# Turning the normalised rows of blocks 1 to 3: TensorE transposes, or a way over memory and 32x32 turns on VectorE

## The chip, the core and the metric

The kernel runs on one core of a Trainium2 chip. The metric is device time in microseconds (us), from runs without a profiler; the profile comes from one separate profiled execution. The engines are PE (TensorE: matmuls and transposes; PEld is its weight load, which overlaps), DVE (VectorE), ACT (ScalarE), POOL (GpSimd) and SP (SyncE, which here only issues DMAs). Each engine works through its own instructions in order; they wait for one another on semaphores.

## What is computed

One block of a transformer on 2048 tokens (S) with 512 features (D), all in float32:

```python
xn = _layernorm(x, axis=-1)
s = _A_ref(xn, A_wqkv, A_wo)
g = _silu(_B_ref(xn, B_w_gate, B_w_up, B_w_down))
return x + s * g
```

`_A_ref` is attention with 32 heads of 16 features and no mask; `_B_ref` is `(silu(x @ w_gate) * (x @ w_up)) @ w_down` with 1792 hidden features. Both take the same normalised rows `xn`. The matrix products contract over the features, and TensorE contracts over the partitions (the 128 rows of on-chip memory), so `xn` is needed with its features on the partitions: it has to be turned.

## The kernel before

**Two phases.** A prologue (lines 446 to 797, about the first 160 us) normalises x, turns it and makes queries, keys and values. Then comes a long loop over attention units (from line 821), into which the feed-forward products and the output projection are dealt as filling work. The change lies in the prologue.

**Blocks, tiles and slots.** The 2048 tokens are 4 blocks (`NB`) of 512 (`TB`); a block has 4 tiles (`NT`) of 128 tokens. For each block b the loop at lines 685 to 762 runs through 12 slots (`n`): 8 of `feature_tile` (line 632), which make 128 rows of queries or keys for all 512 tokens, and 4 of `value_tile` (line 644), which make the values of 128 tokens. Block 0 has the values first (slots 0 to 3), blocks 1 to 3 have them last (slots 8 to 11). Each slot is 12 matmuls, because every operand is split into a high and a low fp32r part and three of the four products are kept (`project`, line 577). The result lies in one of four PSUM buffers `ps`.

**What a feature slot issues.** ACT squares and copies `ps` (lines 637 and 638), DVE takes the difference (line 639), and SP stores both halves, 512 KB, to `q_d` or `k_d` (line 641). `parts` has four buffers. A value slot has one ACT copy into `vt` (line 659).

**The turn of the next block.** While block b is worked on, block b+1 is prepared. `load_x` (line 464) has SP load four tiles of x into `xin`; `stats(t)` (line 530) and `rates` (line 540) make mean and scale on DVE, with one square root on ACT; `norm(t)` (line 551) writes the normalised tile `xn`, 128 tokens by 512 features, into a buffer of tag `ga`, which has two. `turn` (line 558) then issues four TensorE transposes of 128x128 into a PSUM bank, and `split_x` (line 563) has ACT cast the result to the high part (line 565) and DVE take the difference (line 568). They land in `xt[b % 2]`, which the matmuls of the next block read: a feature slot reads all four tiles. After tile 3 POOL stores `xt` to `xt_d` (line 574) for the feed-forward phase. Which slot does what stands in lines 728 to 737: in blocks 1 and 2, x is loaded in slot 1, stats in slots 2 to 5, rates in slot 5, norms in slots 6 to 9, turns in slots 7 to 10. In block 0 the x tiles are loaded in slot 2, stats are made in slots 2 and 3, and rates in slot 4.

**What sets the order.** The order within each engine is the order of the program text (`manual_schedule`, line 53). The Tile layer adds the semaphore waits: a reader waits for its writer, also through DRAM, and a new tile in a buffer waits until all uses of the old one are done. A DMA's waits stand on the engine that issues it, so everything behind it on that engine waits too.

**Other users of what the change touches.** `th` and `wdr` are tags with one buffer of 128x512 floats each (pool `one`). In the prologue `wdr` receives the first rows of the down weights (`load_wd(0)`, line 701, read after the prologue), and `th` serves tile 0 of block 0 (`xf`, line 604) and later the feed-forward products. `load_gu` (line 123) loads gate and up weights, two DMAs of 256 KB, in slots 6 and 7 of block 2. In block 0, `load_w`, `high_w` and `low_w` (lines 690 to 695) still load and split weights, and `copy_fx` (line 667) has ACT copy the turned block 0 into `fx`. `flush` (line 680) reduces the squares; it stands in slot 8 of blocks 1 to 3 and in slot 0 of block 1.

Of the kernel before, what the change touches and what calls it, by code (L numbers as in the profile page):

```python
# [9 lines left out]
F32 = mybir.dt.float32  # L10
# [9 lines left out]
P = 128  # L20
S = 2048
D = 512
# [4 lines left out]
TB = S // NB  # L27
NT = TB // P
# [22 lines left out]
def tile_block(ctx: ExitStack, tc: tile.TileContext, x, wqkv, wo, w_gate, w_up, w_down, out):  # L51
# [3 lines left out]
    mm, act, dve, sp, pool = nc.tensor.matmul, nc.scalar.activation, nc.vector, nc.sync, nc.gpsimd  # L55

    dram = ctx.enter_context(tc.tile_pool(name="dram", bufs=1, space=DRAM))
# [4 lines left out]
    xt_d = dram.tile([NB, 2, P, DT, TB], F32, name="xt_d")  # L62
    g_d = dram.tile([S, D], F32, name="g_d")
    o_d = dram.tile([DT, NB, P, TB], F32, name="o_d")

    const = ctx.enter_context(tc.tile_pool(name="const", bufs=1))
    one = ctx.enter_context(tc.tile_pool(name="one", bufs=1))
    two = ctx.enter_context(tc.tile_pool(name="two", bufs=2))
# [51 lines left out]
    gu, wdr = {}, {}  # L120


    def load_gu(i):
        f = i % NF
        raw = two.tile([P, DC, P], F32, tag="gur", name="gur")
        for j, w in enumerate((w_gate, w_up)):
            sp.dma_start(raw[j * HALF:(j + 1) * HALF], w[:, f * P:(f + 1) * P].rearrange("(c p) f -> p c f", p=HALF))
        gu[i] = [raw]
# [9 lines left out]
    def load_wd(i):  # L138
        raw = one.tile([P, D], F32, tag="wdr", name="wdr")
        sp.dma_start(raw, w_down[(i % NF) * P:(i % NF + 1) * P])  # L140
        wdr[i] = raw
# [304 lines left out]
    with ExitStack() as pro:  # L446
# [10 lines left out]
        def load_tile(t):  # L457
            if t:
                sp.dma_start(xin[:, t % NT], x[t * P:(t + 1) * P])
            else:  # L460
                for engine, w in zip((nc.scalar, sp), wide):
                    engine.dma_start(xin[:, t, w], x[t * P:(t + 1) * P, w])

        def load_x(b):
            for t in range(NT):
                load_tile(b * NT + t)
# [11 lines left out]
        def load_w(m):  # L478
            wraw[m] = two.tile([P, DT, P], F32, tag=("gur", "guh", "gul")[len(wraw) % 3], name="wraw")
            if m < 8:  # L480
                src = wqkv[:, m * P:(m + 1) * P].rearrange("(c p) f -> p c f", p=P)
            else:
                c = m - 8
                src = wqkv[c * P:(c + 1) * P, 2 * D:3 * D].rearrange("p (c f) -> p c f", f=P)
            sp.dma_start(wraw[m], src)
# [6 lines left out]
        def high_w(m):  # L492
            nc.scalar.copy(parts_w(m)[0], wraw[m])

        def low_w(m):
            hi, lo = parts_w(m)
            return pool.tensor_sub(lo, wraw[m], hi.bitcast(F32))
# [30 lines left out]
        xn = {}  # L528
# [22 lines left out]
        def norm(t):  # L551
            xn[t] = two.tile([P, D], F32, tag="ga", name="xn")
            return dve.tensor_scalar(xn[t], xin[:, t], mv[:, t, 0:1], rs[:, t:t + 1], op0=ALU.subtract, op1=ALU.mult)
# [4 lines left out]
        def turn(t):  # L558
            for c in range(DT):
                turn_one(acc[t % 2], t, c)  # L560
            return acc[t % 2].rearrange("p (c f) -> p c f", f=P)

        def split_x(b, t, av, between=None):
            hi, lo = (xt[b % 2][j][:, :, t * P:(t + 1) * P] for j in range(2))
            nc.scalar.copy(hi, av)
            if between:
                between()
            dve.tensor_sub(lo, av, hi.bitcast(F32))  # L568

        def turn_x(b, t, between=None):  # L570
            split_x(b, t, turn(t), between)
            if t == NT - 1 and b:
                for j in range(2):
                    pool.dma_start(xt_d[b, j], xt[b % 2][j].bitcast(F32))

# [109 lines left out]
        for b in range(NB):  # L685
            more = b + 1 < NB
            slots = [(feature_tile, m) for m in range(8)]
            slots = [(value_tile, t) for t in range(NT)] + slots if b == 0 else slots + [(value_tile, t) for t in range(NT)]
            for n, (make, i) in enumerate(slots):
                if b == 0:  # L690
                    if n + 5 < 12:
                        load_w(worder[n + 5])
                    if n >= 2 and n + 2 < 12:
                        high_w(worder[n + 2])
                        low_w(worder[n + 2])
                if n == (1 if b else 2) and more:
                    load_x(b + 1)
                if b == 2 and n in (6, 7):
                    load_gu(n - 6)
                if b == 2 and n == 8:  # L700
                    load_wd(0)
                if not more and n == 2:
                    split_gu(0)
                    for bank in acc:
                        dve.memset(bank, 0.0)
                if not more and n in (1, 3):
                    load_k(0, n // 2)
                if not more and n == 5:
                    load_q(0)
                if not more and n == 6:  # L710
                    for c in range(2):
                        load_v(0, c)
                if b == 0 and n == 1:
                    norm(2)
                    norm(3)
                made = make(b, i)
                if b == 0 and n == 2:
                    split_x(0, 0, xf)
                if b < 2 and 0 <= 12 * b + n - 3 < 16:
                    copy_fx(12 * b + n - 3)  # L720
                if n == 0 and b == 1:
                    flush(0)
                if make is feature_tile:
                    pend.append(made)
                if b == 0 and n == 11:
                    ring(0, 2, one)
                    queries(0, one)
                if more:
                    for t in range(NT):
                        if n == 2 + (t if b else t // 2):  # L730
                            stats(t)
                    if n == (5 if b else 4):
                        rates(0, NT)
                    if 6 <= n < 10:
                        norm(n - 6)
                    if 7 <= n < 11:
                        turn_x(b + 1, n - 7)
                if n == 8 and b:
                    flush(b)
                if not more and n == 8:  # L740
                    dve.reduce_max(pk, peak, axis=AX.X)
                    dve.tensor_add(sm, pk[:, 0:1], pk[:, 1:2])
                if not more and n == 9:
                    tops = pps.tile([P, 512], F32, tag="ps", name="tops")
                    nc.tensor.transpose(tops[0:1, :P], sm, ident)
                    dve.reduce_max(s4, tops[0:1, :P], axis=AX.X)
                    dve.tensor_scalar(s4, s4, 0.51, None, op0=ALU.mult)
                    dve.tensor_scalar(flag, s4, LIMIT, None, op0=ALU.is_le)
                    dve.tensor_scalar(sel[:, :NG * NB], row[:, :NG * NB], s4, None, op0=ALU.mult)
                    for h in range(2):  # L750
                        dve.tensor_copy(selq[:, h * HALF:h * HALF + 1], s4)
                    fill(3 * DC)
                    low, high = [pps.tile([P, 512], F32, tag="ps", name="low") for _ in range(2)]
                    mm(high[:2 * NG * NB, :8], sel, row[:, :8], start=True, stop=True, skip_group_check=True)
                    mm(low[:HALF + 2, :8], selq, row[:, :8], start=True, stop=True, skip_group_check=True)
                    act(shift, high[:2 * NG * NB, 0:1].to_broadcast([2 * NG * NB, 512]), AF.Copy, scale=-1.0)
                    for h in range(2):
                        two_rows = slice(h * HALF, h * HALF + 2)
                        act(qst[0][two_rows], low[two_rows, None, 0:1].to_broadcast([2, 2, 512]), AF.Copy, scale=-1.0)
                    for j in range(4):  # L760
                        pool.dma_start(sh_d[:, j * 512:(j + 1) * 512], shift.bitcast(F32))
                    fast = nc.values_load(flag, min_val=0, max_val=1)


        with tc.If(fast < 1):
            with tc.tile_pool(name="gen", bufs=1) as gen:
                for h in range(2):
                    pool.memset(qst[0][h * HALF:h * HALF + 2].bitcast(F32), 0.0)
                for g in range(NG):
                    for b in range(NB):  # L770
# [3 lines left out]
                        for j in range(NB):  # L774
                            load_k(g, j, j % 2)
                            for i in range(4 * NT):
                                h, t = divmod(i, NT)
                                ps = pps.tile([P, 512], F32, tag="ps", name="ps")
                                r = slice(h % 2 * HALF, h % 2 * HALF + NROW)
# [41 lines left out]
    for u in range(units):  # L821
        g, b = divmod(u, NB)
        q = qst[u % 2]
        for kp in range(steps):
            now = u * steps + kp
            probs = []
            for i in range(2):
# [4 lines left out]
                for j in range(2):  # L832
                    for h in range(2):
                        r = slice(h * HALF, h * HALF + NROW)
# [41 lines left out]
    turned = []  # L876
# [65 lines left out]
```

## Time and profile before

| What | Value |
|---|---|
| median of 3 runs | 1436.54 us (1436.37 to 1437.82) |
| the profiled execution, whole time | 1437.19 us |
| its span, first to last instruction | 1435.4 us |
| granted TensorE clock, mean | 0.999 |
| instructions | 26786 |
| DMA over the span | 149.15 MB, mean 104 GB/s |
| DMA, 0 to 170 us | 39.13 MB, mean 230 GB/s |

How to read the rows that follow. In a timeline a row has the start in us from the span's start, the duration, the engine, the line of the kernel, the operation, output<-inputs, shapes and the number of merged instructions; in brackets the idle time before it and what ended it. SPq is SP issuing: the duration is that of the issue, not of the transfer. Where several are merged, the duration runs from the first one's start to the last one's end. In the rows by group the fields are count | busy us, mean ns of one | idle us before, and what ended it. Rows that begin with A:B are stretches: the width, the granted clock, the share of time in which the 16 DMA engines were busy, and GB/s; where the PE is shown, its busy time and count stand ahead of the clock. "DMA packets" and "q1" tell the packets of a stretch, their MB and the time they took as a share of 16 engines. DMA issues are given with KB each and the median time from issue to landing.

### The profile page before, as it was taken

Reading aid. Unit: us, or ns where it says so; the run is one execution under the profiler, and the core shown is the slowest. Engines: PE = TensorE matmul, PEld = TensorE weight load, DVE = VectorE, ACT = ScalarE, POOL = GpSimd, SP = SyncE. Lnnn points to the kernel's source line nnn. Section 1 sums busy time; section 2 is a strip of 40 time slices with the busy share of each in tenths; the row PEclk is TensorE's granted clock in tenths of the full one; section 3 lists DMA queues with packets and bytes.
Section 4 is the critical chain, followed back from the end, with each engine's and each line's share of the span. In section 5 each row is a group of like instructions: output and inputs, shape, how many; then the busy total and the mean of one; then the engine's idle time right before and its main releaser. Section 6 shows DMA issues by size and latency. Waiting matters only on the chain.

```text
span 1435.4 us, 26786 instructions
## 1 busy us (share of the span) xinstructions
PE 1428.2 (99%) x11221; PEld 803.6 (56%) x11221; DVE 535.0 (37%) x886; ACT 1112.2 (77%) x1236; POOL 89.6 (6%) x103
## 2 busy tenths in 40 slices
PE   9999999999999999999999999999999999999998
PEld 7778655555555555555555555555555555555555
DVE  5543344112523342134323431243344422243665
ACT  6733688888888888788888888888888887888764
POOL 4200200000000000000000000000000000000154
PEclk9999999999999999999999999999999999999999
DMA  7778652032274321142553320342824210412552
GB/s 222 264 242 253 157 119 64 17 96 60 64 153 119 97 65 34 38 105 71 111 134 90 94 49 12 79 104 58 177 79 121 65 42 12 101 30 78 196 183 104
DMA packets 127668, 149.15 MB, mean 104 GB/s; under 512 B 12604, under 2 KB 79676, under 8 KB 126772
## 3 DMA queue, kind: packets, MB, share of 16 engines
q1 hardware_dynamic: 122196, 126.71, 34.5%
q0 software_dynamic: 4912, 20.12, 3.8%
q8 instruction: 91, 1.49, 0.5%
q10 hardware_dynamic: 432, 0.52, 0.1%
q14 instruction: 37, 0.30, 0.1%
HBM read 107.20 MB, written 40.11 MB: 103 GB/s over the span
## 4 chain that ended last, share of the span: by engine, by line
PE 88%; DVE 0%; issue 0%; DVEq 0%
PE acc L356 33%; PE bankx L174 32%; PE score L835 20%; PE banky L174 3%; DVE y L889 0%; PE acc L882 0%; DVE y L895 0%; PE score L882 0%; PE banky L882 0%; DVEq L938 0%; DVE rl L886 0%; DVEq L895 0%
## 5 line engine op out<-in xcount | busy, mean ns | idle before, releaser
L837 ACT ACTIVATE pr<-score 128x1024 f32<-128x1024 f32 x1024 | 993.2, 1023 | 223.0 <-PE score L835 222.4
L356 PE MATMUL acc<-pr,vst 128*17 128x512 f32 x4096 | 489.2, 595 | 0.0
L835 PE MATMUL score<-qst,kst 50*128 50x512 f32 x2048 | 352.1, 421 | 0.0
L835 PEld LDWEIGHTS score<-qst,kst 50*128 50x128 f32 x2048 | 177.1, 184 | 263.7 <-ACT pr L837 225.7
L174 PE MATMUL bankx<-fx,guh 64*128 64x512 f32 x896 | 288.8, 392 | 0.1
L174 PE MATMUL banky<-fx,guh 64*128 64x512 f32 x896 | 288.8, 392 | 0.0
L356 PEld LDWEIGHTS acc<-pr,vst 128*17 128x17 f32 x4096 | 94.0, 96 | 234.6 <-issue 233.8
L204 DVE SCALAR_TENSOR_TENSOR ga<-th,bankx 128x512 f32<-128x512 f32 x56 | 38.5, 688 | 445.3 <-ACT th L203 445.3
L174 PEld LDWEIGHTS bankx<-fx,guh 64*128 64x128 f32 x896 | 165.7, 185 | 34.5 <-issue 0.9
L174 PE MATMUL banky<-fx,gul 64*128 64x512 f32 x448 | 175.3, 391 | 0.0
L174 PE MATMUL bankx<-fx,gul 64*128 64x512 f32 x448 | 175.3, 391 | 0.0
L174 PEld LDWEIGHTS banky<-fx,guh 64*128 64x128 f32 x896 | 165.7, 185 | 2.8
L174 PE MATMUL banky<-wd,hh 64*128 64x512 f32 x672 | 166.7, 389 | 0.0
L174 PE MATMUL bankx<-wd,hh 64*128 64x512 f32 x672 | 166.6, 389 | 0.0
L174 PEld LDWEIGHTS bankx<-wd,hh 64*128 64x128 f32 x672 | 124.0, 185 | 26.1
L174 PEld LDWEIGHTS banky<-wd,hh 64*128 64x128 f32 x672 | 124.0, 185 | 1.4
L174 PEld LDWEIGHTS bankx<-fx,gul 64*128 64x128 f32 x448 | 82.9, 185 | 17.8
L174 PEld LDWEIGHTS banky<-fx,gul 64*128 64x128 f32 x448 | 82.8, 185 | 1.4
L588 PE MATMUL ps<-xt,wh 128*128 128x512 f32 x256 | 80.9, 397 | 0.1
L222 DVE COPY facc<-bankx 128x512 f32<-128x512 f32 x16 | 11.1, 692 | 171.1 <-PE banky L174 150.3
L135 DVE TENSOR_TENSOR gul<-gur,guh 128x1024 fp32r<-128x1024 f32 x56 | 68.6, 1225 | 2.1
L588 PEld LDWEIGHTS ps<-xt,wh 128*128 128x128 f32 x256 | 47.8, 188 | 11.8 <-DVE xt L568 0.5
(161 smaller groups left out, 1019.1 us busy)
## 6 DMA issues: line engine op xcount, KB each, us to landing
gur<-in_B_w_gate_dram SPq DMA_DIRECT2D x56, 256.0 KB
gur<-in_B_w_up_dram SPq DMA_DIRECT2D x56, 256.0 KB
wdr<-in_B_w_down_dram SPq DMA_DIRECT2D x56, 256.0 KB
kst<-k_d SPq DMA_DIRECT2D x192, 64.0 KB
qst<-q_d SPq DMA_DIRECT2D x192, 64.0 KB
fx<-xt_d SPq DMA_DIRECT2D x24, 512.0 KB
q_d<-parts SPq DMA_DIRECT2D x16, 512.0 KB
k_d<-parts SPq DMA_DIRECT2D x16, 512.0 KB
```

The costliest lines, as they stand in the source:

```text
L135: dve.tensor_sub(lo, raw, hi.bitcast(F32))
L174: mm(bank, lhs[h], rhs[h], start=start, stop=stop)
L204: dve.scalar_tensor_tensor(ga, th, 1.0, bankx, op0=ALU.add, op1=ALU.mult)
L222: dve.tensor_copy(facc[:, t], bankx)
L356: mm(a[h * 32:h * 32 + DH + 1], v[:, kt % CT, h * (DH + 1):(h + 1) * (DH + 1)], probs[2 * i + h // 2][:, h % 2], start=kt == 0, stop=kt == ...
L588: mm(ps, w, a[:, c], start=n == 0, stop=n == 3 * DT - 1)
L835: mm(score[j][:, h], k[r, j, kc * P:(kc + 1) * P], q[r, j], start=True, stop=True)
L837: exps.append(act(pr, score[j], AF.Exp, scale=0.25))
```

## The change

The transposes of blocks 1 to 3 are taken from TensorE. Each normalised tile is stored to a new DRAM tensor `xn_d`, in the slot of its `norm`. One slot later four loads (`spread`), 32 partitions each, bring it back with its 32x32 squares already in their turned places: 128 bytes (32 floats) are contiguous in a run, 512 runs to a load. Then DVE turns every 32x32 square where it stands (`turn_over`), and `split_x` works from on-chip memory instead of PSUM. The buffers are `th` and `wdr` in turn for the loaded tile and `ga` for the turned one. The four tiles of block 0 keep the TensorE path.

The slots move: in blocks 1 and 2, x is loaded in slot 0, stats are in slots 1 to 3, rates in slot 3, norms and stores in slots 4 to 7, loads of the squares at the head of slots 5 to 8, turns at the end of slots 7 to 10 as before. In block 0, norms move from slots 6 to 9 to slots 4 to 7. `load_wd(0)` moves to slot 0 of block 3.

```diff
+    xn_d = dram.tile([S, D], F32, name="xn_d")
...
         def turn_x(b, t, between=None):
             split_x(b, t, turn(t), between)
-            if t == NT - 1 and b:
+        xb = {}
+
+        def spread(b, t):
+            xb[t] = one.tile([P, D], F32, tag=("th", "wdr")[t % 2], name="xb")
+            src = xn_d[b * TB + t * P:b * TB + (t + 1) * P].rearrange("(a j) (c g i) -> g j c a i", j=32, g=4, i=32)
+            for g in range(4):
+                dst = xb[t][g * 32:(g + 1) * 32].rearrange("j (c a i) -> j c a i", a=4, i=32)
+                sp.dma_start(dst, src[g])
+
+        def turn_over(b, t):
+            turned = two.tile([P, D], F32, tag="ga", name="turned")
+            dve.transpose(turned, xb.pop(t))
+            split_x(b, t, turned.rearrange("p (c f) -> p c f", f=P))
+            if t == NT - 1:
                 for j in range(2):
                     pool.dma_start(xt_d[b, j], xt[b % 2][j].bitcast(F32))
...
-                if n == (1 if b else 2) and more:
+                if n == (0 if b else 2) and more:
                     load_x(b + 1)
+                if 5 <= n < 9 and more:
+                    spread(b + 1, n - 5)
                 if b == 2 and n in (6, 7):
                     load_gu(n - 6)
-                if b == 2 and n == 8:
+                if b == 3 and n == 0:
                     load_wd(0)
...
                     for t in range(NT):
-                        if n == 2 + (t if b else t // 2):
+                        if n == (1 + (t + 1) // 2 if b else 2 + t // 2):
                             stats(t)
-                    if n == (5 if b else 4):
+                    if n == (3 if b else 4):
                         rates(0, NT)
-                    if 6 <= n < 10:
-                        norm(n - 6)
+                    if 4 <= n < 8:
+                        norm(n - 4)
+                        r = (b + 1) * TB + (n - 4) * P
+                        sp.dma_start(xn_d[r:r + P], xn[n - 4])
                     if 7 <= n < 11:
-                        turn_x(b + 1, n - 7)
+                        turn_over(b + 1, n - 7)
```

## The prediction, made before the changed kernel was run

> **What bounds the kernel now.** I read first the busy times, then the stretch that the change touches (the prologue, 0 to about 160 us) on TensorE's timeline.
>
> ```profile
> PE 1428.2 (99%) x11221; PEld 803.6 (56%) x11221; DVE 535.0 (37%) x886; ACT 1112.2 (77%) x1236; POOL 89.6 (6%) x103
> 22.10 0.62 PE L588 MATMUL ps<-xt,wh 128*128 128x512 f32 x2
> 24.88 0.64 PE L588 MATMUL ps<-xt,wh 128*128 128x512 f32 x2
> 33.25 0.60 PE L556 MATMUL acc<-ident,xn 128*128 128x128 f32 x4
> 36.48 0.60 PE L556 MATMUL acc<-ident,xn 128*128 128x128 f32 x4
> 46.16 1.01 PE L588 MATMUL ps<-xt,wh 128*128 128x512 f32 x2
> 83.25 0.62 PE L588 MATMUL ps<-xt,wh 128*128 128x512 f32 x2
> 119.20 0.62 PE L588 MATMUL ps<-xt,wh 128*128 128x512 f32 x2
> ```
>
> TensorE is busy throughout, so time taken from it is gained and any wait put on it is lost. A slot (one `make`) takes 24.88 - 22.10 = 2.78 us; one with a turn of four transposes takes 36.48 - 33.25 = 3.23. A turn costs 0.45. Blocks 1, 2 and 3 begin at 46.16, 83.25 and 119.20. **Removed:** 12 turns, 12 x 0.45 = 5.4 us. This is all that the change can gain.
>
> **The new path.** A block has 12 slots, 12 x 2.78 = 33.4 us without turns, and the next block's first slot needs all four tiles turned. Each tile now goes: norm on DVE, store of `xn` on SP, four gathers on SP which read what that store wrote, a 32x32 turn on DVE, cast on ACT, difference on DVE. SP issues in program order. It stands still before tile t's gathers until tile t's store has landed; the stores of `parts` and the next tile's `xn` store queue behind. So the tiles follow one another round a loop on SP, and I cost that loop. These are SP's issue times:
>
> ```profile
> 2.64 0.43 SPq L459 DMA_DIRECT2D facc<-in_A_x_dram  x1
> 3.11 0.43 SPq L485 DMA_DIRECT2D wraw<-in_A_wqkv_dram  x1
> 63.25 8.73 SPq L641 DMA_DIRECT2D k_d<-parts  x4
> 88.47 4.43 SPq L459 DMA_DIRECT2D facc<-in_A_x_dram  x4
> 102.45 0.72 SPq L127 DMA_DIRECT2D gur<-in_B_w_gate_dram  x1
> 103.22 0.66 SPq L127 DMA_DIRECT2D gur<-in_B_w_up_dram  x1
> ```
>
> One issue occupies SP 0.47 us (3.11 - 2.64), for a weight tile in 512 runs as for an x tile in 128 rows; a gather has 32 x 16 = 512 runs. Four: 1.9 us. Behind a full queue one takes 4.43 / 4 = 1.1, four 4.4; that is the upper bound.
>
> Packets, in a stretch with 512-byte ones (18 to 22 us) and one with 2 KB ones (65 to 81 us):
>
> ```profile
> DMA packets 925, 0.46 MB, mean 114 GB/s; under 512 B 32, under 2 KB 925, under 8 KB 925
> q1 hardware_dynamic: 925, 0.46, 39.9%
> DMA packets 934, 1.80 MB, mean 112 GB/s; under 512 B 64, under 2 KB 64, under 8 KB 933
> q1 hardware_dynamic: 933, 1.78, 29.4%
> ```
>
> 0.399 x 4 us x 16 / (925 - 32) = 28.6 ns for 512 bytes, and 0.294 x 16 x 16 / (933 - 64) = 87 ns for 2 KB. The line through them gives 14 ns at 128 bytes; a run that costs as much as a 512-byte one gives 28.6. A tile has 2048 runs, 128 for each of 16 engines: 1.8 to 3.7 us. I take 2.6, between them, so that the queue lags the issue (1.9) by 0.7. The Trainium skill (DMA: Bandwidth & Descriptors, Specifications) puts line rate at 512 bytes and up and says that shorter transfers are read, modified and written; no 128-byte run is in this trace, and by the rule a tile would take at least the 3.7, the whole 12 x 1.1 = 13 us more.
>
> Landing of a store that SP waits for:
>
> ```profile
> 0.76 0.39 SPq L462 DMA_DIRECT2D facc<-in_A_x_dram  x1
> 3.54 0.75 DVE L537 BATCH_NORM_STATS2 st<-facc 128x6 f32<-128x256 f32 x2 [0.79 <-DMA facc<-in_A_x_dram]
> 73.50:74.00 0.50, 1.00 0.79 287
> 74.00:74.50 0.50, 1.00 0.00 0
> xt_d<-xt POOLq DMA_DIRECT2D x6, 1024.0 KB, 5.3
> ```
>
> The last `k_d` store goes out at 63.25 + 8.73 - 0.36 = 71.6 and its data flow until about 73.9: 512 KB, 2.3 us after issue, without the acknowledgement. A load of 128 KB is used 3.54 - 0.76 = 2.8 after issue. An `xn` store (256 KB) queues right behind a `parts` store of 512 KB. Bounds 2.3 and 5.3 (xt_d, 1 MB); I take 3.1, by the first two rows. A gather's last quarter lands 2.5 after issue (the 128 KB load less some data), plus the lag of 0.7.
>
> **When the first `xn` store goes out.** DVE's rows:
>
> ```profile
> 28.39 0.80 DVE L549 SCALAR_TENSOR_TENSOR rs<-nw,rs 128x4 f32<-128x4 f32 x1
> 59.75 0.69 DVE L639 TENSOR_TENSOR parts<-ps,parts 128x512 fp32r<-128x512 f32 x1 [0.75 <-ACT parts L638]
> 65.93 0.68 DVE L533 BATCH_NORM_STATS2 st<-facc 128x6 f32<-128x512 f32 x1
> 68.26 0.16 DVE L549 SCALAR_TENSOR_TENSOR rs<-nw,rs 128x4 f32<-128x4 f32 x1
> 95.88 0.67 DVE L639 TENSOR_TENSOR parts<-ps,parts 128x512 fp32r<-128x512 f32 x1
> L553 DVE TENSOR_SCALAR xn<-facc,mv,rs 128x512 f32<-128x512 f32 x16 | 8.5, 539 | 0.1
> L363 DVE STREAM_TRANSPOSE o<-acc 128x512 f32<-128x512 f32 x31 | 22.0, 711 | 19.8 <-PE acc L356 19.8
> L565 ACT CAST xt<-acc 128x512 fp32r<-128x512 f32 x15 | 8.9, 591 | 4.8 <-PE acc L556 4.7
> L568 DVE TENSOR_TENSOR xt<-acc,xt 128x512 fp32r<-128x512 f32 x15 | 10.3, 690 | 14.3 <-ACT xt L565 14.3
> ```
>
> In block 2, slot 3's split ends at about 96.5; the last stats and the rates follow (65.93 to 68.42 in block 1, 2.5; I take 2.4), then slot 4's split (0.6) and norm (0.54): 100.05, which is 16.8 after the block's start. Block 1, from 59.75 by the same steps: 63.9, 17.75 after its start. Block 0: rates end at 29.2, norm at 29.8.
>
> **From there to the last tile.** Four landings 4 x 3.1 = 12.4. Three gathers 3 x 2.6 = 7.8. Three times a `parts` store in between, 3 x 0.45 = 1.35. Then the buffers: `turned` takes a `ga` buffer from an `xn` whose store must have landed, and tile 2's gather names tile 0's `th` (tile 3's names tile 1's `wdr`) before that has been turned; SP waits for both turns, 2 x 0.75 = 1.5. Last gather: three issues 1.4, landing 2.5 + 0.7, together 4.6. Turn, cast, difference: 0.7 + 0.6 + 0.7 = 2.0. Sum 29.65 us.
>
> - Block 1: 17.8 + 29.65 = 47.45, against 83.25 - 46.16 = 37.1: +10.4.
> - Block 2: 16.8 + 29.65 = 46.45; the gate and up loads of slots 6 and 7 stand on SP between a gather and the next `xn` store, 2 x 1.4 (rows above): 49.25, against 119.20 - 83.25 = 35.95: +13.3.
> - Block 0: 29.8 + 29.65 = 59.45, against 46.16: +13.3. Its ACT queue, held at the casts, also has copies of `fx` before the last one; I add one, 1.0: +14.3.
>
> ```profile
> L672 ACT CAST fx<-xt 64x1024 fp32r<-64x1024 f32 x16 | 16.8, 1048 | 0.3
> ```
>
> Together 38.0 us; the removed turns are in it, since the old block times contain them. While DVE waits for a landing, the `flush` reductions and the later turns stand behind it; behind ACT's wait stand the `vt` copies, and in block 0 two weight casts, which delay slots 10 and 11. Four `ps` buffers take four slots, so this ends before the last tile does, at no cost; without that cover each slot adds 2.78.
>
> **The clock.** TensorE now stands still three times, in block 1 for 47.45 - 34 = 13 us.
>
> ```profile
> 1.38 4.21 PE L502 MATMUL acc<-ident 128*128 128x128 f32 x18 [1.38 <-POOL ident masks.py:199]
> 7.34 4.26 PE L623 MATMUL ps<-wraw,xf 128*128 128x512 f32 x6
> 11.88 1.02 PE L623 MATMUL ps<-wraw,xf 128*128 128x512 f32 x2
> 1430.05 0.40 PE L882 MATMUL banky<-fx,rl 128*128 128x512 f32 x1
> 1432.00:1433.50 1.50, 0.00 (x0) 1.00 0.68 254
> 1433.60:1435.40 1.80, 0.00 (x0) 0.50 0.19 65
> ```
>
> The granted clock falls to 0.50 some 3.15 us after the last matmul. At the start, eighteen take 4.21 (0.234 each; four of L556 later take 0.60), and six of L623 take 4.26 against 1.02 for two: the slow clock seems to last to about 10 us, and costs about half of that, 4.4. Bounds 0 and 4.4 for each stall; I take 2.2, 6.6 for three. The Trainium skill (TensorE: Matmul & The Clock Gate, Part 1: The HAM clock gate) has half clock after one idle window of about 3.4 us, and full clock after one busy one; the tail agrees (3.15). By it, an estimate, a stall costs half of 3.4, 1.7, and the three 5.1.
>
> **Edits at nothing.** x loads one slot earlier: on SP they follow the last gather (block 0: the last `parts` store), at least two slots, 5.6 us, ahead of the first stats, against 2.8 from issue to use above; a late one shifts the first norm one for one. The `wdr` load at block 3: its reader runs after the prologue. DVE's 12 turns (8.5 us) lie in the chain above.
>
> **Sum:** the profiled execution's 1437.2 + 38.0 + 6.6 = 1481.8; the median is 0.65 below it: **1481**.
>
> **Rivals.**
> (a) Short waits: landings 2.3, no lag, no slow clock. Per block 4 x 0.8 + 4 x 0.7 = 6.0 less, 18 in all, and 6.6 less: 1456. For it: the data end at 2.3. Against it: an acknowledgement must follow.
> (b) Full queue: gathers at 4.4 instead of 2.6, 12 x 1.8 = 22 more: 1503. For it: 88.47, when a block's stores and x loads meet; against it: from slot 4 on the 2 KB stretch is idle between stores (0 GB/s at 74).
> (c) Short runs written twice: 2 x 28.6 ns, 7.3 a tile instead of 2.6, 12 x 4.7 = 56 more: 1537. No row speaks for it. It is what the rule of the Trainium skill named above (DMA: Bandwidth & Descriptors) could mean.
> (d) Not slower: the path stays under the old blocks. It decides where the loop from the first store to the last tile takes under 35.95 - 16.8 = 19.2 instead of 29.65, so that a landing takes 3.1 - 10.4 / 4 = 0.5 us; then 1436.5 - 5.4 = 1431. Against it: no transfer shown is used within 2.3.
> (e) The stall only balances the gain: about 1437.
>
> **How the numbers follow.** Forecast 55%, (a) 20, (b) 13, (c) 6, (d) 4, (e) 2. The range goes from 10 us below (a) to 13 above (b), 1446 to 1516. What this kernel's measurement can tell from no change is about 0.2%, 3 us: faster 0.04, same 0.02, slower 0.94.
>
> **What would show it.** Right: no L556 in blocks 0 to 2 beyond the first tiles; TensorE idle for some 13 us before the blocks 1, 2 and 3, released by DVE's last difference; SP waiting for `xn_d` landings near 3 us and for DVE's turns; blocks starting near 60, 110 and 162. Wrong: block starts as before or earlier; SP's waits under 1 us; idle time of TensorE inside the slots instead of at the block's end; a difference outside the prologue.

## The result, and the profile after

| | before | after |
|---|---|---|
| median, us | 1436.45 (4 runs) | 1488.36 (4 runs, 1487.83 to 1489.68) |
| ratio, 95% interval | | 1.036 (1.0347 to 1.0373) |
| span of the profiled execution, us | 1435.4 | 1486.0 |
| start of blocks 1, 2, 3, us | 46.16, 83.25, 119.20 | 59.12, 109.85, 166.87 |

The kernel became 52 us slower; 1481 had been forecast. In the changed kernel the lines are shifted: the products of a slot stand in L605 (L588 before), the TensorE turn in L557, the cast and the difference of the turned tile in L566 and L569. New are the gathers in L583, the turn on VectorE in L587 and the store of `xn` in L756.

The span in 40 slices on the profile's page, after (busy share of TensorE and its granted clock, in tenths):

```profile
PE   9669599999999999999999999999999999999998
PEclk9889799999999999999999999999999999999999
```

One slice is 37 us. TensorE falls under 9 in the second, third and fifth slice and the granted clock falls with it; the later slices are full up to the last. Of the 50.6 us by which the span grew, 47.7 are there when block 3 starts (166.87 - 119.20). Of the 2.9 that come later, 2.6 are the half of the slow stretch of 5.2 us told below, so next to nothing lies outside the prologue.

TensorE's timeline of the changed kernel, at the starts of the blocks (the first row is slot 10 of block 0):

```profile
47.23 1.22 PE L605 MATMUL ps<-xt,wh 128*128 128x512 f32 x2 [8.92 <-ACT wh L494]
59.12 0.52 PE L605 MATMUL ps<-xt,wh 128*128 128x512 f32 x1 [3.31 <-ACT xt L566]
109.85 1.52 PE L605 MATMUL ps<-xt,wh 128*128 128x512 f32 x2 [13.56 <-ACT xt L566]
166.87 1.52 PE L605 MATMUL ps<-xt,wh 128*128 128x512 f32 x2 [20.37 <-ACT xt L566]
```

The stalls stand in front of the blocks and not inside the slots, each released by the split of the last tile: by ACT's cast, not by the difference on VectorE that had been forecast. In block 0 the stall is divided: ACT holds two weight casts (L494) behind its own wait for a turned tile, so slots 10 and 11 run late, and only the rest of the wait, 3.31, is left in front of block 1.

SP's timeline, blocks 1 and 2. The first three rows are one turn of the loop: the store of `xn`, the four gathers that wait for it, the store of `parts` behind them.

```profile
78.50 0.42 SPq L756 DMA_DIRECT2D xn_d<-xn  x1
81.62 2.61 SPq L583 DMA_DIRECT2D xb<-xn_d  x4
84.33 0.57 SPq L658 DMA_DIRECT2D k_d<-parts  x1
85.00 0.41 SPq L756 DMA_DIRECT2D xn_d<-xn  x1
88.20 2.61 SPq L583 DMA_DIRECT2D xb<-xn_d  x4
...
95.93 2.61 SPq L583 DMA_DIRECT2D xb<-xn_d  x4
...
102.94 2.60 SPq L583 DMA_DIRECT2D xb<-xn_d  x4
128.73 0.41 SPq L756 DMA_DIRECT2D xn_d<-xn  x1
...
141.68 0.69 SPq L128 DMA_DIRECT2D gur<-in_B_w_gate_dram  x1
...
143.75 0.47 SPq L756 DMA_DIRECT2D xn_d<-xn  x1
150.09 2.65 SPq L583 DMA_DIRECT2D xb<-xn_d  x4
...
154.86 0.47 SPq L756 DMA_DIRECT2D xn_d<-xn  x1
160.31 2.65 SPq L583 DMA_DIRECT2D xb<-xn_d  x4
```

In block 1 the first two stores are followed by their gathers after 3.1 and 3.2 us (81.62 - 78.50, 88.20 - 85.00), the other two after 4.4 and 3.7, and one turn of the loop takes 6.6, 7.7 and 7.0 us. In block 2, behind the loads of the gate and up weights, the time from a store to its gathers is 6.3 and 5.5 us (150.09 - 143.75, 160.31 - 154.86). Of the 6.3 the store's landing took 5.6: VectorE's timeline has its next turn released by it, and SP's gathers name that turn's buffer and follow it.

```profile
149.35 0.71 DVE L587 STREAM_TRANSPOSE turned<-xb 128x512 f32<-128x512 f32 x1 [9.87 <-DMA xn_d<-xn]
```

What a landing consists of is told by the stretch behind the store of 85.00:

```profile
85.50:87.50 2.00, 1.00 1.06 386
```

At 386 GB/s, 2.0 us are the time of 768 KB: the 512 KB of the `parts` store at 84.33 and the 256 KB of `xn` behind it. The gathers follow 0.7 us later, at 88.20. The first store of block 0, at 29.11, has no `parts` store right ahead (the last went out at 26.22), and its gathers follow after 2.1 us, at 31.20.

Waits of SP, ACT and TensorE over the first 200 us (total us, times, longest):

```profile
SPq L583 <- DMA xn_d<-xn: 36.6, 12, 5.1
ACT xt L566 <- DVE turned L587: 62.1, 12, 14.4
PE ps L605 <- ACT xt L566: 37.2, 3, 20.4
```

SP stood before the gathers of all twelve tiles, 36.6 us in all; ACT's casts waited 62.1 us for VectorE's turns; TensorE's three waits in front of the blocks sum to 37.2.

Stretches with TensorE's busy time (count), its granted clock, the DMA share and GB/s:

```profile
59.00:63.00 4.00, 3.67 (x9) 0.57 1.06 385
110.00:120.00 10.00, 10.00 (x35) 0.80 0.93 350
167.00:172.00 5.00, 5.00 (x11) 0.50 0.93 326
170.00:175.00 5.00, 5.00 (x19) 0.79 1.00 380
```

After each stall TensorE resumes at 0.50. A clock of 0.57 over 4 us is 3.4 us at half; 0.80 over 10 is 4.0; 0.50 to 172 and 0.79 over the 5 us from 170 (2.1 at half) put the end of the third at 172.1, 5.2 after its start. Half of the sum, 6.3 us, is lost. The wait of 8.92 in block 0 has a slow stretch behind it too (mean clock 0.53 from 47 to 53 us), but slots 10 and 11 end at 55.8, ahead of the tile that comes at 59.12, so it costs nothing.

The packets of a stretch that holds gathers alone (82 to 84 us):

```profile
DMA packets 769, 0.10 MB, mean 48 GB/s; under 512 B 769, under 2 KB 769, under 8 KB 769
q1 hardware_dynamic: 769, 0.10, 30.4%
```

0.304 x 2 us x 16 / 769 = 12.7 ns for a run of 128 bytes.

### The profile page after: what moved, and what is told of

Its sections match the earlier page's. It is cut to its first block, busy times and chain, and to the rows that moved or that the text cites. A ratio compares the mean times of both kernels' runs of the same rounds, so it can differ in the third digit from the quotient of the medians.

```text
span 1486.0 us, 26811 instructions
## 1 busy us (share of the span) xinstructions
PE 1431.6 (96%) x11173; PEld 802.6 (54%) x11173; DVE 544.8 (37%) x898; ACT 1112.0 (75%) x1236; POOL 89.2 (6%) x103
## 4 chain that ended last, share of the span: by engine, by line
PE 85%; DVE 0%; issue 0%; DVEq 0%
PE acc L357 32%; PE bankx L175 30%; PE score L856 20%; PE banky L175 3%; DVE y L910 0%; PE acc L903 0%; DVE y L916 0%; PE score L903 0%; PE banky L903 0%; DVEq L959 0%; DVE rl L907 0%; DVEq L916 0%
## 5 line engine op out<-in xcount | busy, mean ns | idle before, releaser
L605 PE MATMUL ps<-xt,wh 128*128 128x512 f32 x256 | 87.7, 424 | 46.4 <-ACT xt L566 37.2
L175 PEld LDWEIGHTS bankx<-fx,gul 64*128 64x128 f32 x448 | 82.9, 185 | 17.8
L605 PEld LDWEIGHTS ps<-xt,wh 128*128 128x128 f32 x256 | 51.7, 203 | 61.9 <-ACT xt L566 38.6
```

What stands on the lines that cost most here:

```text
L175: mm(bank, lhs[h], rhs[h], start=start, stop=stop)
L605: mm(ps, w, a[:, c], start=n == 0, stop=n == 3 * DT - 1)
```

## The experiments

The theory is the one of the prediction: the loop on SP (store, landing, gathers, next store) is longer than what a block hides, and TensorE's clock adds to it. Its rivals: the short runs themselves; the moved slots; the buffers; a general slowing of the queue, against which the rest of the kernel, nearly unchanged in length, already speaks. Diffs are against the changed kernel unless said otherwise; each ratio is to the kernel before, with its 95% interval.

**Take the landing out of SP's way.** The gathers stand one slot later, so that each `xn` store has a slot more in which to land.

```diff
-                if 5 <= n < 9 and more:
-                    spread(b + 1, n - 5)
+                if 6 <= n < 10 and more:
+                    spread(b + 1, n - 6)
```

> The gathers of the squares stand at the head of slots 6 to 9 instead of 5 to 8, so that on SP the next tile's store goes out before SP waits for this tile's landing. Theory (SP goes round a loop of store, landing, gather for each tile): the landing is now under the next slot's work, the loop falls from some 6.7 us a tile to gathers 2.65 + two stores 1.2 = 3.9, the blocks end some 10 us earlier, TensorE's wait at the block's end falls from 13 us to about 4 and most of the slow clock goes: 1453 us, 1444 to 1465. Rival (the 128-byte runs or the memory itself are slow, whatever the order): no tile comes sooner, each gather starts a slot later: 1488 to 1497.

Measured: 1458.47 us (1457.63 to 1459.45), ratio 1.0151 (1.0134 to 1.0168), 30 us less than the changed kernel. SP's wait for the landings (first 170 us) and block 2's start on TensorE's timeline:

```profile
SPq L583 <- DMA xn_d<-xn: 2.0, 2, 1.4
```

```profile
90.32 1.52 PE L605 MATMUL ps<-xt,wh 128*128 128x512 f32 x2 [3.71 <-ACT xt L566]
```

36.6 us of waiting have become 2.0, and block 2 starts 19.5 us earlier. Every tile still takes the same steps; only SP's standing still between them is gone.

**Do the slots alone.** TensorE's turns are kept, with no store, gather or turn on VectorE; the norms are back in slots 6 to 9; the loads of x, the stats and `wdr` stay where the change put them.

```diff
-                if 5 <= n < 9 and more:
-                    spread(b + 1, n - 5)
...
-                    if 4 <= n < 8:
-                        norm(n - 4)
-                        r = (b + 1) * TB + (n - 4) * P
-                        sp.dma_start(xn_d[r:r + P], xn[n - 4])
+                    if 6 <= n < 10:
+                        norm(n - 6)
                     if 7 <= n < 11:
-                        turn_over(b + 1, n - 7)
+                        turn_x(b + 1, n - 7)
+                        if n == 10:
+                            for j in range(2):
+                                pool.dma_start(xt_d[b + 1, j], xt[(b + 1) % 2][j].bitcast(F32))
```

> The turns stay on TensorE, with the norms in slots 6 to 9; only the x loads (slot 0), the stats (slots 1 to 3), the rates (slot 3) and the down-weight load (block 3) stand where the change puts them. Theory: these moves cost nothing, 1436 us, 1434 to 1439. Rival (the earlier x loads collide with the block's first stores and the stats hold DVE up): 1440 or more, and part of the 52 us is theirs.

Measured: 1436.47 us (10 runs), ratio 0.9999 (0.9989 to 1.0009). Those moves cost nothing. The earlier norms are not in this run.

**Keep TensorE busy in its waits.** Multiplications of the identity fill the stalls; they go to no output.

```diff
+        WARM = {(0, 10): 36, (1, 0): 14, (2, 0): 54, (3, 0): 84}
...
+                for _ in range(WARM.get((b, n), 0)):
+                    mm(acc[1][:, :P], ident, ident, start=True, stop=True)
```

> The changed kernel, with transposes of the identity added where TensorE waits (36 ahead of slot 10 of block 0, 14, 54 and 84 ahead of blocks 1, 2 and 3), into a PSUM bank that nothing reads. Theory: SP's loop sets the block's end, so the added work is free, and only the slow clock after the waits goes: about half of 3.4, 4.2 and 5.2 us and some of block 0's: 7 us less, 1481 us, 1478 to 1484. If the clock costs nothing: 1488. If TensorE were the bound there: over 1500.

Measured: 1481.57 us (1479.88 to 1483.24), ratio 1.0306 (1.0289 to 1.0323), mean granted clock 0.999 instead of 0.983. By the medians the slow clock is worth 1488.36 - 1481.57 = 6.8 us. The filling did not always hold: two of the four runs had a clock of 1.000 and took 1479.88 and 1480.44, two had 0.999 and took 1482.70 and 1483.24. The profiled one is of the second kind, and its TensorE resumes slowly in front of block 2 (0.72 from 108 to 114 us). Against the mean of the first two, 1480.2, the slow clock is worth some 8 us.

**Undo the short runs.** The same four loads bring whole rows of 2 KB, so that a tile is not turned across its squares.

```diff
-            src = xn_d[b * TB + t * P:b * TB + (t + 1) * P].rearrange("(a j) (c g i) -> g j c a i", j=32, g=4, i=32)
+            src = xn_d[b * TB + t * P:b * TB + (t + 1) * P]
...
-                dst = xb[t][g * 32:(g + 1) * 32].rearrange("j (c a i) -> j c a i", a=4, i=32)
-                sp.dma_start(dst, src[g])
+                sp.dma_start(xb[t][g * 32:(g + 1) * 32], src[g * 32:(g + 1) * 32])
```

> The four loads of a tile bring back plain rows of 2 KB (32 partitions each) instead of 128-byte squares, so that the tile isn't turned across its squares; all else stays. Theory: only the issue gets shorter, from 0.68 to about 0.45 us each, and the landing by 0.3: some 1.2 us a tile, 4 x 3 x 1.2 = 14 less, 1474 us, 1465 to 1481. Rival (the 128-byte runs are the price): most of the 52 us goes, under 1455.

Measured: 1468.41 us (1467.88 to 1470.04), ratio 1.0217 (1.02 to 1.0234), 6 us under the expected value though inside its range. SP's timeline of this run, tile 1 of block 1 and the next store:

```profile
77.68 0.41 SPq L755 DMA_DIRECT2D xn_d<-xn  x1
80.86 1.70 SPq L582 DMA_DIRECT2D xb<-xn_d  x4
...
83.14 0.41 SPq L755 DMA_DIRECT2D xn_d<-xn  x1
```

Four loads are issued in 1.70 us instead of 2.61 and a turn of the loop takes 5.5 instead of 6.6, but the wait of 3.2 for the landing is the same. Without the short runs 20 of the 52 us go, and the loop, though shorter, still makes TensorE wait in front of every block. The 20 and the 30 of the first experiment are not two shares of one sum: the time of the issue, which the short runs lengthen, is itself a part of each turn.

**Move the weight loads of block 2.**

```diff
-                if b == 2 and n in (6, 7):
-                    load_gu(n - 6)
+                if b == 2 and n in (9, 10):
+                    load_gu(n - 9)
```

> The changed kernel with the gate and up loads of block 2 moved from slots 6 and 7, between a gather and the next xn store, to slots 9 and 10, behind all gathers. Theory: in block 2 each of the two xn stores no longer queues behind 512 KB of weights (their landings took 5.5 us there against 3.1 to 3.7 in block 1) and SP doesn't issue them in between (1.4 each): block 2 gets as long as block 1, some 6.7 us shorter: 1481.5 us, 1479 to 1484. Rival (block 2 is longer for another reason, such as its xt_d stores): 1487 or more.

Measured: 1480.69 us (1477.99 to 1481.16), ratio 1.03 (1.0284 to 1.0316). SP's timeline of this run:

```profile
143.84 0.41 SPq L756 DMA_DIRECT2D xn_d<-xn  x1
147.93 2.61 SPq L583 DMA_DIRECT2D xb<-xn_d  x4
...
151.25 0.47 SPq L756 DMA_DIRECT2D xn_d<-xn  x1
154.86 2.61 SPq L583 DMA_DIRECT2D xb<-xn_d  x4
```

The landings are back at 4.1 and 3.6 us. In the changed kernel the two pairs of loads cost 1488.36 - 1480.69 = 7.7 us by the medians; in the traces block 2 takes 50.3 us instead of 57.0 (from 110.58 to 160.86; from 109.85 to 166.87), 6.7 less.

**Give the turned tile buffers of its own.**

```diff
-            turned = two.tile([P, D], F32, tag="ga", name="turned")
+            turned = two.tile([P, D], F32, tag="guh", name="turned")
```

> The changed kernel with the turned tile in buffers of another tag (guh), so that a turn no longer waits for a buffer of xn and SP's third gather no longer waits for that turn. Theory: the buffers are a small term; SP waits 0.9 us less for the first turn in each block, the landing that it waits for anyway stays: 2 to 3 us less, 1485.5 us, 1483 to 1488. Rival (the shared buffers are what makes the stall): the waits of DVE for the xn stores' landing, up to 6 to 10 us a block, go, and the kernel falls under 1470.

Measured: 1483.2 us (1481.95 to 1484.17), ratio 1.0324 (1.0308 to 1.034): 5.2 us less, at the lower end of the expected range. In this trace SP's gathers no longer wait for a turn.

**Issue the stores of `xn` from another engine.** The gathers still wait on SP, but the next store no longer stands behind them.

```diff
-                        sp.dma_start(xn_d[r:r + P], xn[n - 4])
+                        pool.dma_start(xn_d[r:r + P], xn[n - 4])
```

> The changed kernel with the xn stores issued by POOL instead of SP, the gathers left on SP in the slots of the change. Theory: a store now goes out as soon as its norm is done and lands while SP issues the gathers before it; SP's loop falls to gathers 2.65 + a parts store 0.6 and some rest of the landing: the blocks end about 10 us earlier, as with the later gathers: 1456 us, 1447 to 1467. Rival (order on SP plays no part): 1485 to 1490.

Measured: 1456.11 us (1455.16 to 1457.88), ratio 1.0139 (1.0124 to 1.0155). POOL's timeline of this run, block 1:

```profile
74.93 0.54 POOL L756 DMA_DIRECT2D xn_d<-xn  x1 [2.23 <-DVE xn L554]
77.72 0.54 POOL L756 DMA_DIRECT2D xn_d<-xn  x1 [2.26 <-DVE xn L554]
```

The stores now leave 2.8 us apart, the length of a slot, and not 6.5 (85.00 - 78.50). This edit and the later gathers open the loop in two different ways and both gain 30 to 32 us.

**Share the gathers between two queues.** ACT issues two of each tile's four.

```diff
-                    spread(b + 1, n - 5)
+                    spread(b + 1, n - 5, sp, range(2))
...
+                if 5 <= n < 9 and more:
+                    spread(b + 1, n - 5, nc.scalar, range(2, 4))
```

> The changed kernel with half of each tile's gathers issued by ACT, behind the slot's square and copies, instead of SP. In best_a eight gathers shared by SP and ACT took as long as eight on SP alone. Theory: the queues share what makes the runs' descriptors, so the issue of four gathers takes 2.6 us however they are dealt out; SP's loop stays and ACT is held up: 1486 us, 1482 to 1492. Rival (each queue makes its own): 1.3 us less a tile, 12 x 1.3 = 16 us less: 1472, 1468 to 1477.

Measured: 1486.05 us (1484.31 to 1486.69), ratio 1.0343 (1.0328 to 1.0357). The time is the expected one, but its reason, that the two engines share one maker of short runs, is not what the trace shows. SP's timeline of this run, ACT's, the packets from 83.9 to 85.1 us, and the stretch behind them:

```profile
82.43 1.24 SPq L584 DMA_DIRECT2D xb<-xn_d  x2
...
84.44 0.42 SPq L759 DMA_DIRECT2D xn_d<-xn  x1
88.41 1.24 SPq L584 DMA_DIRECT2D xb<-xn_d  x2
```

```profile
82.44 1.51 ACTq L584 DMA_DIRECT2D xb<-xn_d  x2
```

```profile
DMA packets 1436, 0.18 MB, mean 149 GB/s; under 512 B 1436, under 2 KB 1436, under 8 KB 1436
q1 hardware_dynamic: 876, 0.11, 58.3%
q10 hardware_dynamic: 560, 0.07, 37.6%
```

```profile
85.50:87.75 2.25, 1.00 1.08 366
```

The two engines issue side by side: four gathers in 1.5 us instead of 2.6, and the DMA engines are then 96% busy with runs of (0.583 + 0.376) x 1.2 us x 16 / 1436 = 12.8 ns. But the next store, issued at 84.44, is answered at 88.41, 4.0 us later instead of 3.2; this turn of the loop takes 6.0 us instead of 6.6. What is saved in the issue is mostly waited for again at the landing, and the stretches tell how. The store goes out 2.0 us after the first gather instead of 3.4 (84.44 - 82.43, 85.00 - 81.62), but in both kernels the gathers' data begin to move only some 1.4 us after the first issue and the data of the two stores come behind them, here from 85.5 to 87.9 us. A store issued sooner stands longer behind those data. The Trainium skill (DMA: Bandwidth & Descriptors, Issuing engines are not separate DMA queues) says that issuing from several engines saves the time of the issue alone. The trace agrees: SP's issue fell by 1.4 us a tile (2.61 - 1.24), and no more than that was gained, 2.3 us in all.

**Towards a version that loses nothing.** Block 0, which has the least room, goes back to TensorE's turns. In blocks 1 and 2 the norms and stores go in pairs to slots 4 and 5, the gathers to slots 6 and 8, half of them on ACT, and the gate and up loads to slots 9 and 10 of block 2. The core of the diff:

```diff
+                if b and more and n in (6, 8):
+                    for t in (n - 6, n - 5):
+                        spread(b + 1, t, sp, range(2))
...
+                    if b and n in (4, 5):
+                        for t in (2 * n - 8, 2 * n - 7):
+                            norm(t, ("guh", "gul")[t % 2])
...
+                    if b and n in (6, 8):
+                        for t in (n - 6, n - 5):
+                            spread(b + 1, t, nc.scalar, range(2, 4))
+                    if b and n in (7, 9, 10):
+                        for t in {7: (0, 1), 9: (2,), 10: (3,)}[n]:
+                            turn_over(b + 1, t)
```

> Block 0 turns block 1's rows on TensorE, as before. Blocks 1 and 2 take the way over memory with all four norms and stores in slots 4 and 5 (xn in four buffers of tags guh and gul), half of each tile's gathers issued by SP and half by ACT in slots 6 and 8, the turns in slots 7, 7, 9 and 10, and the gate and up loads behind them. Theory: first store 17 us after a block's start, all four landed by 22, the last gather landed by about 31, the last tile turned by 33 of the block's 33.4: no wait of TensorE is left and 8 turns x 0.45 are gained: 1433 us, 1431.5 to 1436. Rival (the way over memory can't be hidden, since stores and gathers collide or ACT is held up): 1437 or more.

Measured: 1446.44 us (1444.81 to 1447.85), ratio 1.0067 (1.0053 to 1.0081): over the expected range and in that of the rival. On SP's timeline, then on ACT's:

```profile
67.91 4.64 SPq L588 DMA_DIRECT2D xb<-xn_d  x4
```

```profile
66.91 0.67 ACTq L588 DMA_DIRECT2D xb<-xn_d  x1
...
67.62 2.80 ACTq L588 DMA_DIRECT2D xb<-xn_d  x3
```

With eight gathers in a row the second queue gains nothing: they take 5.6 us (from 66.91, when ACT issued its first, to 67.91 + 4.64 = 72.55), 0.7 each, as one queue alone needs (5.5 to 6.3 us for eight in the next version). The DMA engines are busy throughout that stretch, a share of 1.02 from 66.91 to 72.55 us, with the gathers and the stores issued before them, which would leave a second issuer nothing idle to use; that is read from the trace and was not tested. And ACT's squares and casts stand behind its share. TensorE still waited 4.15 us before block 2 (at 84.82) and 3.05 before block 3.

**Everything two slots earlier, the gathers on SP alone,** x loaded in slot 10 of the block before, and some copies of `fx` moved. The core, against the version just told:

```diff
-                if b and more and n in (6, 8):
-                    for t in (n - 6, n - 5):
-                        spread(b + 1, t, sp, range(2))
+                if b and more and n in (4, 6):
+                    for t in (n - 4, n - 3):
+                        spread(b + 1, t, sp, range(4))
...
-                    if b and n in (4, 5):
-                        for t in (2 * n - 8, 2 * n - 7):
+                    if b and n in (2, 3):
+                        for t in (2 * n - 4, 2 * n - 3):
...
-                    if b and n in (6, 8):
-                        for t in (n - 6, n - 5):
-                            spread(b + 1, t, nc.scalar, range(2, 4))
-                    if b and n in (7, 9, 10):
-                        for t in {7: (0, 1), 9: (2,), 10: (3,)}[n]:
+                    if b and n in (5, 7, 8):
+                        for t in {5: (0, 1), 7: (2,), 8: (3,)}[n]:
```

> As best_a (block 0 on TensorE, four buffers for xn), with the gathers all on SP and everything two slots earlier: the x tiles of blocks 2 and 3 are loaded in slot 10 of the block before, stats in slots 0 and 1, rates in slot 1, norms and stores in slots 2 and 3, gathers at the head of slots 4 and 6, turns in slots 5, 5, 7 and 8; ACT's copies of fx in block 1 go two to a slot. Theory: SP's loop starts 5.6 us earlier and ends about 30 us after the block's start, ahead of 33.4: TensorE no longer waits and 8 turns x 0.45 = 3.6 us are gained: 1432.8 us, 1431.5 to 1434.5. Rival (contention or held-up queues take it back): 1436 or more.

Its control has the same slots with TensorE's turns in place of stores, gathers and VectorE's turns:

```diff
-                if b and more and n in (4, 6):
-                    for t in (n - 4, n - 3):
-                        spread(b + 1, t, sp, range(4))
...
-                            r = (b + 1) * TB + t * P
-                            sp.dma_start(xn_d[r:r + P], xn[t])
...
-                            turn_over(b + 1, t)
+                            turn_x(b + 1, t)
```

> The control to best_b: the same slots, buffers and loads, but no stores and gathers, and the turns on TensorE in slots 5, 5, 7 and 8. Theory: as before the change, 1436.4 us, 1435 to 1438, so that best_b's gain is that of the turns. If it falls with best_b, the gain is that of the earlier loads.

Measured: 1435.35 us with the way over memory (0.9993, 0.9984 to 1.0002), 1436.28 us for the control (1.0001, 0.9992 to 1.001), 11 runs each. The first is over its expected range and under its rival's. No block waits any more, yet of the eight removed turns, 8 x 0.45 = 3.6 us, only 0.9 shows, and the first interval still holds no change. TensorE's timeline of the first of the two:

```profile
72.78 0.38 PE L616 MATMUL banky<-sq,ind 128*32 128x512 bf16 x1 [0.60 <-ACT sq L658]
```

The reduction of the squares (`flush`, slot 8) waits for squares that ACT holds behind its casts. In the control's trace the same products start without a wait, so moving them would have nothing to gain there; the control was not run with them moved.

**The same with `flush` two slots later in blocks 1 and 2.**

```diff
-                if n == 8 and b:
+                if b and n == (10 if more else 8):
```

> best_b with the flush of the squares in blocks 1 and 2 moved from slot 8 to slot 10. In best_b TensorE's squares waited about 1.0 us in each of these blocks for ACT's squares, which stood behind casts held for a landing; with the spacing of the squares this is 2.26 us against the control. Theory: with it gone, the eight turns' 3.5 us come out whole: 1433.0 us, 1432.0 to 1434.5. Rival (the rest of the gain is lost elsewhere): 1435 to 1436.

Measured: 1434.67 us (11 runs, 1433.56 to 1437.06), ratio 0.9988 (0.9979 to 0.9997): 1.7 us under the kernel before, the only version under it with its whole interval, though by little, and 0.2 above the expected range. TensorE's timeline of the control at the end of block 3, then of this version:

```profile
146.80 0.39 PE L611 MATMUL ps<-vl,xt 128*128 128x512 f32 x1
```

```profile
143.89 0.39 PE L611 MATMUL ps<-vl,xt 128*128 128x512 f32 x1
145.18 0.27 PE L782 MATMUL tops<-ident,sm 128*1 128x128 f32 x1 [0.90 <-DVE sm L779]
```

At the last product of the prologue this version is 2.9 us ahead (146.80 - 143.89); 0.4 of that stands already at the start of block 1 (45.26 and 44.83), before any removed turn, so that some 2.5 of the 3.6 belong to the turns. Then TensorE waits for VectorE, and the next product, at 145.18, is only 1.9 ahead of the control's (147.03). ACT's timeline and SP's tell why:

```profile
142.24 0.59 ACT L659 CAST parts<-ps 128x512 fp32r<-128x512 f32 x1 [3.62 <-DMA q_d<-parts]
```

```profile
112.69 0.85 SPq L128 DMA_DIRECT2D gur<-in_B_w_gate_dram  x1
...
120.74 9.54 SPq L101 DMA_DIRECT2D kst<-k_d  x6
130.61 1.70 SPq L662 DMA_DIRECT2D q_d<-parts  x2
```

The gathers push the weight loads to 112.7 us (108.1 in the control). The loads of keys behind them take 9.54 us to issue (3.32 in the control), the `parts` stores behind those leave late, and ACT's cast waits for a free `parts` buffer; VectorE's last difference and the reductions follow it. Part of the gain is given back on the same queue, one block later. This chain is read from the trace; moving those loads was not tried.

## Why the prediction was right

It was right in direction and in its mechanism, and near in size: 1481 forecast, 1488.36 measured. That the sum came so near owes something to small errors of both signs. Step by step:

- **What bounds it.** Right. The blocks' starts, forecast at 60, 110 and 162, came at 59.1, 109.9 and 166.9, and the stalls stand before the blocks.
- **The loop on SP.** Right, and shown twice: with the landing out of SP's way, or with the store off SP, 30 to 32 us vanish. From the first `xn` store to the next block it takes 30.0 us in block 0 (from 29.11), 31.4 in block 1 (109.85 - 78.50); the sum was 29.65.
- **First stores.** In block 0 the first store was forecast at 29.8 us and went out at 29.11. In blocks 1 and 2 it went out 19.4 and 18.9 us after the block's start, against 17.8 and 16.8. The slow clock explains only a part: in the run that keeps TensorE busy, where block 1 begins at the full clock, it is still 18.5 there (58.73 to 77.20).
- **Terms of the loop.** The landing was taken as 3.1. In block 1 the first two took 3.1 and 3.2; the third took 3.6 and 0.7 more for the turn that SP waits for; the fourth took 3.7. Four gathers with their lag were taken as 2.6: the issue alone takes 2.61, because one issue takes 0.65 and not 0.47. The lag did not vanish beside it: from the first issue of the last four to the turn of that tile it was 5.5 us (102.94 to 108.43), 4.6 forecast. Cast and difference were charged in full, and TensorE started on the cast. The line through the two packet sizes gave 14 ns for 128 bytes; 12.7 were measured.
- **Gate and up loads in block 2: mis-sized.** This is the term that carries the error. The prediction charged 2 x 1.4 = 2.8 us for their issue. Moving them away gave 7.7 (6.7 by the length of block 2). The issue was sized rightly, 1.4 to 1.5 a pair. What was left out is their data: 512 KB of each pair lie ahead of the `xn` store, whose landing took 5.5 to 5.6 us instead of 3.1. From first store to block 3 it was 38.1 us (166.87 - 128.73) against a forecast 32.45: 5.7 too little, of the 6.0 between the forecast of the profiled execution, 1481.8, and its time, 1487.83. The other errors nearly cancel: block 1 started 1.3 us before its forecast and was 1.1 longer.
- **The clock.** 6.6 was forecast for three stalls; 6.8 were measured by the medians and some 8 with the clock at 1.000. The slow stretches were 3.4, 4.0 and 5.2 us long. The rule of the Trainium skill that was weighed (TensorE: Matmul & The Clock Gate, Part 1: The HAM clock gate) has full clock after one busy window of about 3.4 us, and the estimate from it was 5.1 for the three; only the first stretch is that short. The same section says that the window is free-running, so that the change depends on where in it the work begins; stretches of different length agree with that, and no run here shows the window itself.
- **Buffers.** 2 x 0.75 for each of three blocks, 4.5; giving `turned` its own buffers returned 5.2. The size is right, the way to it only in part: SP waited for a turn four times in the three blocks, 2.8 us in all, where six times 0.75 had been charged. Where the rest of the 5.2 comes from is not shown.
- **Edits at nothing.** Right: the moved x loads, stats and `wdr` cost nothing (0.9999). The held weight casts in block 0 delayed slots 10 and 11, which ended before the last tile came, as foreseen.
- **The rivals.** (a) falls with the landings, 3.1 and more behind a `parts` store (2.1 once without one), and with the clock. (b) falls with gathers of 2.6 instead of 4.4. (c) falls with 12.7 ns: no read-and-write of short runs shows in these loads, and the Trainium skill's 512 bytes (DMA: Bandwidth & Descriptors, Specifications) put no such price on them here. (d) needed a loop under 19.2 and (e) a stall of the size of the gain; neither came near.
- **Removed turns.** 12 x 0.45 = 5.4 is the least tested figure. In the best version some 2.5 of the 3.6 us for eight turns were still there at the end of block 3.

## What to carry to other kernels

A store whose result is read back by the same in-order queue closes a loop: its length is issue, landing and issue again, and everything else on that queue, its bytes too, counts in each turn. Put the reader so many steps behind the writer that it never stands and waits, or put the two on different queues; here either gained 30 to 32 us of the 52. When a DMA stands ahead of a store that someone waits for, charge the time of its data and not only that of its issue.

## What the runs showed that had not been expected

- A gather of 512 runs of 128 bytes takes 0.65 us to issue (2.61 for four), a load of the same 64 KB in 2 KB rows 0.43 (1.70 for four). Before, 0.47 had been seen for 512 runs of 512 bytes.
- Two queues issued four gathers in 1.5 us, but eight in 5.6. While the eight went out, the DMA engines were busy all the time (1.02); whether that alone makes the second figure no better than one queue's is open.
- Runs of 128 bytes, 12.7 to 12.8 ns each, lie close to the line through the larger packets: there is no floor at the price of 512 bytes. A tile of 2048 runs takes 2048 x 12.8 / 16 = 1.6 us of the DMA engines, less than its issue.
